# Three raw weight chunks in flight in a fused attention and two-layer-MLP kernel, with its conversion buffers placed elsewhere

## The chip, the cores and the metric

The kernel runs on one core of one Trainium2 chip. The metric is the device time of one execution in microseconds (us); before the change the median of three timed runs is 530.14 us.

## The reference

Attention with a tanh cap over 2 x 12 heads, 448 tokens, head size 64; then a layer of 1024 columns with a softmax gate and a layer norm; then a gated layer of 1536 columns. The weights arrive as 64-bit floats.

```python
scores = cap * np.tanh(scale * np.matmul(q, kT) / cap)
attn = np.exp(scores - max); attn = attn / (sum + 1e-09)
x = np.matmul(attn, v)                      # -> [896, 768]
h = x @ w_in                                # 768 -> 1024
solu = h * softmax(h)
x = (layernorm(solu) * g_ln) @ w_out        # 1024 -> 768
gate = sigmoid(x @ w_gate); val = x @ w_val # 768 -> 1536 each
out = gate * val @ w_out2                   # 1536 -> 768
```

## The kernel before

Four stages follow one another on TensorE (PE): attention with the start of the first layer beside it, the rest of the first layer, the second layer, the gated layer with the output product. Matmuls of the layers are done three times each, on a high and a low part of both operands (`hi`, `lo`).

**Attention.** The heads go in 12 pairs, each pair in two halves, so there are 24 *slots* (the loop over `s`, L533). In a slot ScalarE (ACT) takes the tanh of two tiles (L197), then their exp (L219); below, tanh 0 to tanh 23 number the slots by their tanh. PE does the scores of a half (`s_mm`, L191, 8 matmuls with both chunks), the product with v (`s_pv`, L237) and the sums of the exponentials (L245; for the pairs of `ADD_PAIRS`, 9 and 10, VectorE (DVE) first adds two tiles, L231, and PE sums half as often, L243). After a pair `s_out` copies the sums (DVE, L252) and the output (ACT, L253, tile `to`, 2 buffers), sends the sums through DMAs (L258); `n_recip` inverts them and spreads them over the partitions by two more DMAs (L266, L268); `n_mult` (GpSimd, POOL, L272) multiplies `to` by them two pairs later and so frees its buffer.

**Weights.** A chunk is 128 x 768 words of 64 bits (768 KB). `chunk_load` (L307) has the SP queue load it into `wraw` (2 buffers). Five word steps (L332 or, on ACT, L330; then on DVE L335, L336, L337, L338) make a 32-bit float out of it; L338 is the last reader of the raw chunk. The 8 chunks of `w_in` go through `cvt` and are split by L352 (ACT) and L355 (DVE); the 8 chunks of `w_mid` are made in place in tiles of the pool `w2a`. `chunk_stream` lays the steps of neighbouring chunks over each other:

```python
            steps[n - 1 - delay] = lambda f=f, c=c: (f(), load(c + AHEAD))
            order += [(n // 2 * c + k + (k >= n - delay), c, step) for k, step in enumerate(steps)]
```

For `w_mid` (five steps, delay 0) this puts step 5 of chunk c (L338) and the load of chunk c + AHEAD at the place of step 1 (L330) of chunk c + 2. `fill` hands the steps out evenly over the slots: `w_in` over slots 0 to S_WI, `w_mid` from S_WI to S_W2.

**Order.** PE, ACT, DVE and POOL run in the order in which the program names their instructions (`manual_schedule`, L459) up to L678; SP's order and everything behind L678 is the scheduler's. An engine works strictly in order.

**First layer.** Seven tiles of 128 tokens. Two run inside the attention, in thirds of 12 matmuls (L405): tile 0 in slots 17 to 19, tile 1 in slots 20 to 22. PSUM has three `big` buffers; scores take two in each slot, an accumulating tile takes one, and its buffer comes free only when DVE has done L423 (L415 max, L420 exp on ACT, L423 product). After the attention, tiles 2 to 6 go one by one.

**Gated layer.** `load_slabs` (L680) loads and converts two chunks (a *slab* each) for each of 12 steps, two steps ahead (`w4p`, 6 buffers; `w3p` for the first two), through `cvt` again; a step is 72 matmuls (L635). The output product has 6 steps of the same kind.

Of the kernel before, what the change touches and what calls it, by code (L numbers as in the profile page):

```python
# [20 lines left out]
P = 128  # L21
# [21 lines left out]
N_RAW = 3  # L43
AHEAD = 2

W2_EARLY = 4

ADD_PAIRS = range(9, 11)

# [3 lines left out]

S_WI = 14
S_W2 = 22
# [24 lines left out]
def fused_kernel(ctx: ExitStack, tc: tile.TileContext, qk, v, cap, w_in, w_mid, g_ln, w_gv, w_fin, outT):  # L80
# [4 lines left out]
    sh.pso = ctx.enter_context(tc.tile_pool(name="pso", bufs=2, space=PSUM))  # L85
    sh.wraw = ctx.enter_context(tc.tile_pool(name="wraw", bufs=2, side="right"))
    sh.cvt = ctx.enter_context(tc.tile_pool(name="cvt", bufs=2, side="right"))
    sh.dram = ctx.enter_context(tc.tile_pool(name="dram", bufs=2, space=DRAM))
# [52 lines left out]
def network(ctx: ExitStack, tc: tile.TileContext, sh, general, w_in, w_mid, w_gv, w_fin, outT):  # L141
    nc = tc.nc
    wide = w_in.dtype != F32
    wraw, cvt, ps, pso, ident = sh.wraw, sh.cvt, sh.ps, sh.pso, sh.ident
    sfx = "_g" if general else ""
# [11 lines left out]

    lin2 = lns.enter_context(tc.tile_pool(name="lin2" + sfx, bufs=2, side="right"))
    wi, x0 = ExitStack(), ExitStack()
    wip = wi.enter_context(tc.tile_pool(name="wi" + sfx, bufs=1, side="left"))  # L160
    x1p = wi.enter_context(tc.tile_pool(name="x1" + sfx, bufs=1, side="left"))
    x0p = x0.enter_context(tc.tile_pool(name="x0" + sfx, bufs=1, side="left"))
    wi_hi = wip.tile([P, 2, K1, 512], F32R, name="wi_hi")
# [57 lines left out]
    def s_pv(i, u):  # L221

        if u == 0:
            outs[i] = pso.tile([P, 512], F32, tag="o", name="o"), pso.tile([P, 512], F32, tag="o", name="sums")
        o, sums = outs[i]
        e = [es.pop((2 * i + j, u)) for j in range(2)]
        add = i in ADD_PAIRS and not general
        if add:
            for j in range(2):
                t = a3.tile([KC, S], F32, tag="es", name="es", bufs=4)  # L230
                nc.vector.tensor_tensor(t, e[j][:, 0], e[j][:, 1], ALU.add)  # L231
                es_sums.append(t)
        for c in range(2):
            kc = 2 * u + c
            for j in range(2):
                d = slice(j * D, j * D + D)
                nc.tensor.matmul(o[d, :S], vs[i][:, kc, d], e[j][:, c], start=(kc == 0), stop=(kc == 3))  # L237
        if add and u == 0:
            return
        for k in range(4):  # L240
            d = slice(k * 32, (k + 1) * 32)
            if add:
                nc.tensor.matmul(sums[d, :S], sh.ones, es_sums[k // 2 + k % 2 * 2], start=True, stop=True)  # L243
            else:
                nc.tensor.matmul(sums[d, :S], sh.ones, e[k // 2][:, k % 2], start=(u == 0), stop=(u == 1))  # L245
        es_sums.clear()

    def s_out(i):
        o, sums = outs.pop(i)
        t = a2.tile([P, S], F32, tag="to", name="to")  # L250
        st = a2.tile([P, S], F32, tag="ts", name="ts", bufs=1)
        (nc.vector.tensor_copy if i < NPAIR - 1 else nc.scalar.copy)(st, sums[:, :S])  # L252
        nc.scalar.copy(t, o[:, :S])  # L253
        tos[i] = t, st
        if i < NPAIR - 1:
            rs[i] = a2.tile([2 * RP, 2, RN], F32, tag="r", name="r")
            for c in range(2):
                nc.sync.dma_start(out=rs[i][:, c], in_=st[32 * c::D].rearrange("j (p n) -> j p n", n=RN))  # L258
# [14 lines left out]

    last, es_sums = {}, []

# [64 lines left out]

    def chunk_steps(get, dst, act=False):

        st = {}

        def place():
            st["w"] = cvt.tile([P, CH], U32, tag="cvt", name="cvt")
            return st["w"]
# [126 lines left out]
    wi_srcs = [w_in[:, c * CH:(c + 1) * CH] for c in range(K1 * F1 // CH)]  # L474
    chunk_stream(wi_srcs, lambda c, get: chunk_steps(get, wi_dst(c)), 1)

# [56 lines left out]
    for s in range(-1, NS):  # L533
# [25 lines left out]
        for first, end in ((0, S_WI), (S_WI, S_W2)):  # L559
            if first <= s < end:  # L560
                fill(-(-len(todo) // (end - s)))
        if u and i >= 2:
            n_mult(i - 2)
        if u and s > 0 and i < NPAIR - 1:
# [5 lines left out]
        if u == 0:  # L570
            v_load(i + 1)
        else:
            if i >= 1:
                n_recip(i - 1)
        if s < NS - 1:
            phase(s, 2)
            phase(s, 3)
# [102 lines left out]
    def load_slabs(src, pool):  # L680
# [3 lines left out]
        for c in range(src.shape[1] * P // CH):  # L684
            hl = pool.tile([P, 2, CH // P, P], F32R, tag="w", name="w_hl")
            parts = hl[:, 0].rearrange("p a b -> p (a b)"), hl[:, 1].rearrange("p a b -> p (a b)")
            r = chunk_load(flat[:, c * CH:(c + 1) * CH])
            for step in chunk_steps(lambda: r, lambda: parts, act=True):
                step()
            out.append(hl)  # L690
# [5 lines left out]


    w3p = ctx.enter_context(tc.tile_pool(name="w3p" + sfx, bufs=2, side="left", reuse_waits="tile"))
    w3 = [load_slabs(w_gv[0], w3p)]
    lns.close()  # L700
    w4p = ctx.enter_context(tc.tile_pool(name="w4p" + sfx, bufs=6, side="right", reuse_waits="tile"))
    w3 += [load_slabs(w_gv[1], w4p)]
# [73 lines left out]
```

## Time and profile before

| | us |
|---|---|
| median of three timed runs | 530.14 |
| lowest and highest of them | 528.61 and 530.21 |
| profiled execution: its time | 528.39 |
| profiled execution: its span | 526.5 |
| PE busy in the span | 499.9 (95%) |
| DVE busy | 312.0 (59%) |
| ACT busy | 234.6 (45%) |
| POOL busy | 55.8 (11%) |

All times of instructions are counted from the span's start; the execution's own time is 1.9 us longer than its span. Shares of the whole span say little here, since the four stages have different limits; they are read stage by stage.

### The profile page before, as it was taken

The numbers are of one execution on the slowest core, as the hardware profiler recorded it, in microseconds if no ns is written. First come the engines' busy times: TensorE is split into PE (matmuls) and PEld (weight loads), VectorE is DVE, ScalarE is ACT, GpSimd is POOL, SyncE is SP. The second block draws the span as 40 slices with busy tenths as digits, with TensorE's granted clock in tenths as the row PEclk, the third lists the DMA queues.
The fourth block names the chain that finished last, engine by engine and source line by source line (L and its number), as shares of the span: only waits on it lengthen the run. The fifth ranks groups of instructions, "written<-read, shape, count | busy, mean of one in ns | idle before, by whom it ended". The sixth has DMA issues, their size and how long they took to land.

```text
span 526.5 us, 6251 instructions
## 1 busy us (share of the span) xinstructions
PE 499.9 (95%) x2480; PEld 386.6 (73%) x2480; DVE 312.0 (59%) x424; ACT 234.6 (45%) x288; POOL 55.8 (11%) x41
## 2 busy tenths in 40 slices
PE   8998998879789889999999999999999999999996
PEld 4332232435366668988899999999999999999995
DVE  0776556659967779321189988776667675551000
ACT  5998996667524545120154433333333333332000
POOL 0011100002221110000001111111101111000000
PEclk9999998998999999999999999999999999999999
DMA  7567645442620000300033453333332234400001
GB/s 268 171 186 219 216 142 187 150 140 78 194 82 1 0 2 0 121 0 1 0 117 124 132 168 121 119 121 120 121 115 82 104 121 138 154 37 22 33 35 40
DMA packets 15313, 55.03 MB, mean 105 GB/s; under 512 B 2796, under 2 KB 5740, under 8 KB 15276
## 3 DMA queue, kind: packets, MB, share of 16 engines
q1 hardware_dynamic: 15276, 54.56, 32.3%
q8 instruction: 21, 0.34, 0.3%
q14 instruction: 16, 0.13, 0.1%
HBM read 51.68 MB, written 2.79 MB: 103 GB/s over the span
## 4 chain that ended last, share of the span: by engine, by line
PE 67%; DVE 12%; ACT 11%; DMA 6%; issue 2%; POOL 1%; SPq 0%; ACTq 0%; POOLq 0%; DVEq 0%
PE big L635 36%; PE l4o L635 16%; PE l2o L635 8%; DMA w_raw<-in_w_mid 4%; ACT e L197 4%; ACT e L219 3%; PE o L237 2%; DVE e L423 1%; PE big L191 1%; PE big L405 1%; DVE st L415 1%; DVE w_lo L527 1%; ACT e L441 1%; ACT e L420 1%; DVE lnlo L456 1%
## 5 line engine op out<-in xcount | busy, mean ns | idle before, releaser
L635 PE MATMUL big<-y_hi,w_hl 128*128 128x448 f32 x576 | 162.2, 362 | 0.0
L635 PEld LDWEIGHTS big<-y_hi,w_hl 128*128 128x128 f32 x576 | 108.0, 187 | 7.0
L635 PE MATMUL big<-y_lo,w_hl 128*128 128x448 f32 x288 | 104.5, 363 | 0.0
L635 PE MATMUL l4o<-p_hi,w_hl 128*128 128x448 f32 x288 | 80.7, 362 | 0.0
L635 PEld LDWEIGHTS big<-y_lo,w_hl 128*128 128x128 f32 x288 | 54.1, 188 | 4.5
L635 PEld LDWEIGHTS l4o<-p_hi,w_hl 128*128 128x128 f32 x288 | 54.0, 187 | 3.3
L355 DVE TENSOR_TENSOR w_hl<-cvt,w_hl 128x768 fp32r<-128x768 f32 x36 | 35.6, 993 | 32.0 <-ACT w_hl L352 31.8
L635 PE MATMUL l4o<-p_lo,w_hl 128*128 128x448 f32 x144 | 52.0, 362 | 0.0
L335 DVE TENSOR_SCALAR cvt<-cvt 128x768 f32<-128x768 f32 x44 | 36.4, 829 | 23.7 <-ACT cvt L330 23.2
L352 ACT CAST w_hl<-cvt 128x768 fp32r<-128x768 f32 x36 | 29.7, 831 | 45.6 <-PE big L635 30.3
L197 ACT ACTIVATE e<-big,cap_inv 112x896 f32<-112x896 f32 x48 | 46.0, 1018 | 6.0 <-PE big L191 5.9
L237 PE MATMUL o<-e,v 112*64 112x448 f32 x192 | 44.7, 556 | 3.7 <-ACT to L253 3.5
L219 ACT ACTIVATE e<-e,cap_abs 112x896 f32<-112x896 f32 x48 | 47.6, 1054 | 0.0
L725 POOL TENSOR_TENSOR p_lo<-sg,p_hi 128x896 fp32r<-128x896 f32 x12 | 25.8, 2153 | 203.3 <-ACT p_hi L724 203.3
L191 PE MATMUL big<-qk_raw 64*112 64x448 f32 x192 | 45.8, 578 | 1.0 <-DVE st L429 0.7
L330 ACT ACTIVATE cvt<-w_raw 128x768 f32<-128x768 f32 x36 | 32.2, 900 | 31.3 <-DVE w_hl L355 15.6
L337 DVE SCALAR_TENSOR_TENSOR cvt<-w_raw,cvt 128x768 uint32<-128x768 uint32 x44 | 43.0, 979 | 1.0
L338 DVE SCALAR_TENSOR_TENSOR cvt<-w_raw,cvt 128x768 uint32<-128x768 uint32 x44 | 42.9, 978 | 1.0
L191 PEld LDWEIGHTS big<-qk_raw 64*112 64x112 f32 x192 | 17.0, 179 | 28.3 <-issue 20.9
L405 PE MATMUL big<-wi_hi,xl 128*128 128x512 f32 x84 | 33.8, 402 | 4.1 <-POOL xl L393 3.3
L237 PEld LDWEIGHTS o<-e,v 112*64 112x64 f32 x192 | 13.6, 136 | 31.5 <-ACT e L219 13.3
L405 PE MATMUL big<-wi_hi,xh 128*128 128x512 f32 x84 | 34.7, 413 | 1.7 <-ACT xh L392 1.7
(98 smaller groups left out, 607.5 us busy)
## 6 DMA issues: line engine op xcount, KB each, us to landing
w_raw<-in_w_gv SPq DMA_DIRECT2D x24, 768.0 KB, 4.7
w_raw<-in_w_fin SPq DMA_DIRECT2D x12, 768.0 KB, 4.3
w_raw<-in_w_in SPq DMA_DIRECT2D x8, 768.0 KB, 5.9
w_raw<-in_w_mid SPq DMA_DIRECT2D x8, 768.0 KB, 4.6
qk_raw<-in_qk SPq DMA_DIRECT2D x12, 448.0 KB, 5.5
v<-in_v SPq DMA_DIRECT2D x12, 224.0 KB, 2.6
out_t<-ob SPq DMA_DIRECT2D x12, 224.0 KB, 2.3
qk_raw<-rd SPq DMA_DIRECT2D x22, 112.0 KB, 3.2
```

The source lines that it names most:

```text
L191: nc.tensor.matmul(sc[j][:KC, c, :S], r[d, 1, kc * KC:(kc + 1) * KC], r[d, 0], start=True, stop=True)
L197: nc.scalar.activation(e, es[n, u][:KC, :, :S], AF.Tanh, scale=sh.cap_inv[:KC])
L219: nc.scalar.activation(es[n, u], es[n, u], AF.Exp, scale=sh.cap_abs[:KC])
L237: nc.tensor.matmul(o[d, :S], vs[i][:, kc, d], e[j][:, c], start=(kc == 0), stop=(kc == 3))
L330: first = lambda t, lo, hi: nc.scalar.activation(f32(t), f32(hi), AF.Abs)
L335: word(lambda t, lo, hi: v.tensor_scalar(f32(t), f32(t), as_f32(W_MOST), as_f32(W_LEAST), ALU.min, ALU.max)),
L337: word(lambda t, lo, hi: v.scalar_tensor_tensor(t, hi, TOP, t, ALU.bitwise_and, ALU.bitwise_or)),
L338: word(lambda t, lo, hi: v.scalar_tensor_tensor(t, lo, 29, t, ALU.logical_shift_right, ALU.bitwise_or)),
L352: nc.scalar.copy(st["hi"], st["w"])
L355: nc.vector.tensor_tensor(st["lo"], st["w"], f32(st["hi"]), ALU.subtract)
L405: nc.tensor.matmul(hts[t][:, half], l[:, kk], r[:, half, kk], start=(kk == 0 and m == 0), stop=(kk == K1 - 1 and m == 2))
L635: nc.tensor.matmul(out, l, r, start=(first and m == 0), stop=(last and m == 2))
```

## The change

- `wraw` gets 3 buffers in place of 2, and `AHEAD` is 3 in place of 2, so that three raw chunks can be loaded or waiting.
- `cvt` is no longer one pool for the whole kernel. The `w_in` chunks are converted in tiles of `w2a`, which the `w_mid` chunks use later. The gated layer has a `cvt` of its own, which lies where the first layer's weights lay and so can be written only after the last matmul that reads those.
- `lin2` (tiles of the first layer) moves to the left side of SBUF and is freed with the first layer's weights; `w4p` has 5 buffers in place of 6.
- `ADD_PAIRS` goes: all pairs sum their exponentials on PE.
- `to` has 3 buffers in place of 2, and `n_mult` is named after `n_recip` in its slot.
- `S_WI` is 13 in place of 14: `w_in` is done, and `w_mid` begun, a slot earlier.

```diff
--- before.py
+++ after.py
@@ -41,17 +41,15 @@
 
 N_E = 5
 N_RAW = 3
-AHEAD = 2
+AHEAD = 3
 
 W2_EARLY = 4
-
-ADD_PAIRS = range(9, 11)
 
 L1_BESIDE = 2
 S_L1 = 16
 L1_SLOTS = 3
 
-S_WI = 14
+S_WI = 13
 S_W2 = 22
 WARM = 20
 ORDERED = {mybir.EngineType.PE, mybir.EngineType.Activation, mybir.EngineType.DVE, mybir.EngineType.Pool}
@@ -83,8 +81,7 @@
     const = ctx.enter_context(tc.tile_pool(name="const", bufs=1))
     sh.ps = ctx.enter_context(tc.tile_pool(name="ps", bufs=3, space=PSUM))
     sh.pso = ctx.enter_context(tc.tile_pool(name="pso", bufs=2, space=PSUM))
-    sh.wraw = ctx.enter_context(tc.tile_pool(name="wraw", bufs=2, side="right"))
-    sh.cvt = ctx.enter_context(tc.tile_pool(name="cvt", bufs=2, side="right"))
+    sh.wraw = ctx.enter_context(tc.tile_pool(name="wraw", bufs=3, side="right"))
     sh.dram = ctx.enter_context(tc.tile_pool(name="dram", bufs=2, space=DRAM))
 
 
@@ -141,7 +138,7 @@
 def network(ctx: ExitStack, tc: tile.TileContext, sh, general, w_in, w_mid, w_gv, w_fin, outT):
     nc = tc.nc
     wide = w_in.dtype != F32
-    wraw, cvt, ps, pso, ident = sh.wraw, sh.cvt, sh.ps, sh.pso, sh.ident
+    wraw, ps, pso, ident = sh.wraw, sh.ps, sh.pso, sh.ident
     sfx = "_g" if general else ""
 
     def big():
@@ -155,10 +152,10 @@
     ln_hi[0] = lnt1.tile([P, K2, G1], F32R, name="lnhi0")
     ln_lo[0] = lnt1.tile([P, K2, G1], F32R, name="lnlo0")
 
-    lin2 = lns.enter_context(tc.tile_pool(name="lin2" + sfx, bufs=2, side="right"))
     wi, x0 = ExitStack(), ExitStack()
     wip = wi.enter_context(tc.tile_pool(name="wi" + sfx, bufs=1, side="left"))
     x1p = wi.enter_context(tc.tile_pool(name="x1" + sfx, bufs=1, side="left"))
+    lin2 = wi.enter_context(tc.tile_pool(name="lin2" + sfx, bufs=2, side="left"))
     x0p = x0.enter_context(tc.tile_pool(name="x0" + sfx, bufs=1, side="left"))
     wi_hi = wip.tile([P, 2, K1, 512], F32R, name="wi_hi")
     wi_lo = wip.tile([P, 2, K1, 512], F32R, name="wi_lo")
@@ -224,30 +221,18 @@
             outs[i] = pso.tile([P, 512], F32, tag="o", name="o"), pso.tile([P, 512], F32, tag="o", name="sums")
         o, sums = outs[i]
         e = [es.pop((2 * i + j, u)) for j in range(2)]
-        add = i in ADD_PAIRS and not general
-        if add:
-            for j in range(2):
-                t = a3.tile([KC, S], F32, tag="es", name="es", bufs=4)
-                nc.vector.tensor_tensor(t, e[j][:, 0], e[j][:, 1], ALU.add)
-                es_sums.append(t)
         for c in range(2):
             kc = 2 * u + c
             for j in range(2):
                 d = slice(j * D, j * D + D)
                 nc.tensor.matmul(o[d, :S], vs[i][:, kc, d], e[j][:, c], start=(kc == 0), stop=(kc == 3))
-        if add and u == 0:
-            return
         for k in range(4):
             d = slice(k * 32, (k + 1) * 32)
-            if add:
-                nc.tensor.matmul(sums[d, :S], sh.ones, es_sums[k // 2 + k % 2 * 2], start=True, stop=True)
-            else:
-                nc.tensor.matmul(sums[d, :S], sh.ones, e[k // 2][:, k % 2], start=(u == 0), stop=(u == 1))
-        es_sums.clear()
+            nc.tensor.matmul(sums[d, :S], sh.ones, e[k // 2][:, k % 2], start=(u == 0), stop=(u == 1))
 
     def s_out(i):
         o, sums = outs.pop(i)
-        t = a2.tile([P, S], F32, tag="to", name="to")
+        t = a2.tile([P, S], F32, tag="to", name="to", bufs=3)
         st = a2.tile([P, S], F32, tag="ts", name="ts", bufs=1)
         (nc.vector.tensor_copy if i < NPAIR - 1 else nc.scalar.copy)(st, sums[:, :S])
         nc.scalar.copy(t, o[:, :S])
@@ -271,7 +256,7 @@
         b, hp = divmod(i, NP)
         nc.gpsimd.tensor_tensor(x_sb[b][:, hp], tos.pop(i)[0], sh.first[i % 2][:, 0], ALU.mult)
 
-    last, es_sums = {}, []
+    last = {}
 
     def n_by_pe(i, step):
 
@@ -338,12 +323,12 @@
             word(lambda t, lo, hi: v.scalar_tensor_tensor(t, lo, 29, t, ALU.logical_shift_right, ALU.bitwise_or)),
         ]
 
-    def chunk_steps(get, dst, act=False):
+    def chunk_steps(get, dst, pool, act=False):
 
         st = {}
 
         def place():
-            st["w"] = cvt.tile([P, CH], U32, tag="cvt", name="cvt")
+            st["w"] = pool.tile([P, CH], U32, tag="w", name="w_32")
             return st["w"]
 
         def upper():
@@ -472,7 +457,7 @@
         raws[i] = sh.first[i]
         load_qk(i + 2)
     wi_srcs = [w_in[:, c * CH:(c + 1) * CH] for c in range(K1 * F1 // CH)]
-    chunk_stream(wi_srcs, lambda c, get: chunk_steps(get, wi_dst(c)), 1)
+    chunk_stream(wi_srcs, lambda c, get: chunk_steps(get, wi_dst(c), w2a), 1)
 
 
     beside = {}
@@ -559,8 +544,6 @@
         for first, end in ((0, S_WI), (S_WI, S_W2)):
             if first <= s < end:
                 fill(-(-len(todo) // (end - s)))
-        if u and i >= 2:
-            n_mult(i - 2)
         if u and s > 0 and i < NPAIR - 1:
             s_out(i)
         if m % 2 and m < NS:
@@ -572,6 +555,8 @@
         else:
             if i >= 1:
                 n_recip(i - 1)
+            if i >= 2:
+                n_mult(i - 2)
         if s < NS - 1:
             phase(s, 2)
             phase(s, 3)
@@ -685,7 +670,7 @@
             hl = pool.tile([P, 2, CH // P, P], F32R, tag="w", name="w_hl")
             parts = hl[:, 0].rearrange("p a b -> p (a b)"), hl[:, 1].rearrange("p a b -> p (a b)")
             r = chunk_load(flat[:, c * CH:(c + 1) * CH])
-            for step in chunk_steps(lambda: r, lambda: parts, act=True):
+            for step in chunk_steps(lambda: r, lambda: parts, cvt, act=True):
                 step()
             out.append(hl)
         return out
@@ -695,10 +680,11 @@
         return [w[k // n][:, z, k % n] for z in range(2)]
 
 
+    cvt = ctx.enter_context(tc.tile_pool(name="cvt" + sfx, bufs=2, side="left", reuse_waits="tile"))
     w3p = ctx.enter_context(tc.tile_pool(name="w3p" + sfx, bufs=2, side="left", reuse_waits="tile"))
     w3 = [load_slabs(w_gv[0], w3p)]
     lns.close()
-    w4p = ctx.enter_context(tc.tile_pool(name="w4p" + sfx, bufs=6, side="right", reuse_waits="tile"))
+    w4p = ctx.enter_context(tc.tile_pool(name="w4p" + sfx, bufs=5, side="right", reuse_waits="tile"))
     w3 += [load_slabs(w_gv[1], w4p)]
     ptp = ctx.enter_context(tc.tile_pool(name="ptp" + sfx, bufs=1, side="left", reuse_waits="tile"))
     p_hi = ptp.tile([P, K4, NT], F32R, name="p_hi")
```

**The order of instructions.** The line numbers of the changed kernel are 3 to 15 lower (L197 is L194 there, L253 is L238, L310 is L295, L330 is L315, L335 is L320, L338 is L323, L423 is L408); names are the same.

SP's queue around the last `w_mid` loads. Before, from the sixth load (two loads in the first row) to the next sums behind the first gated loads:

```order
L310 DMA w_raw<-in_w_mid 128x1536 x2
L181 DMA v<-in_v 112x512
L258 DMA r<-ts 16x1x56 x2
L266 DMA rd<-r 16x56
L268 DMA qk_raw<-rd 64x448 x2
L310 DMA w_raw<-in_w_mid 128x1536
L310 DMA w_raw<-in_w_gv 128x1536 x2
L258 DMA r<-ts 16x1x56 x2
```

After, from the sixth load:

```order
L295 DMA w_raw<-in_w_mid 128x1536
L253 DMA qk_raw<-rd 64x448 x2
L95 DMA qk_raw<-in_qk 128x896
L295 DMA w_raw<-in_w_mid 128x1536
L178 DMA v<-in_v 112x512
L243 DMA r<-ts 16x1x56 x2
L251 DMA rd<-r 16x56
L253 DMA qk_raw<-rd 64x448 x2
L295 DMA w_raw<-in_w_mid 128x1536
L178 DMA v<-in_v 112x512
L295 DMA w_raw<-in_w_gv 128x1536
L243 DMA r<-ts 16x1x56 x2
```

The last load of `w_mid` moves from behind the last pair's v load and a pair's sums to ahead of that v load.

ACT around tanh 16, the slot in which the `w_mid` stream first needs ACT. Before, from tanh 14 to the start of tanh 17:

```order
L197 ACTIVATE e<-big,cap_inv 112x896 x2
L219 ACTIVATE e<-e,cap_abs 112x896 x2
L352 CAST wi_hi<-cvt 128x768
L253 COPY to<-o 128x448
L197 ACTIVATE e<-big,cap_inv 112x896 x2
L219 ACTIVATE e<-e,cap_abs 112x896 x2
L197 ACTIVATE e<-big,cap_inv 112x896 x2
L219 ACTIVATE e<-e,cap_abs 112x896 x2
L330 ACTIVATE w_w<-w_raw 128x768
L253 COPY to<-o 128x448
L197 ACTIVATE e<-big,cap_inv 112x896 x2
```

After, from the cast ahead of tanh 14 to the start of tanh 17:

```order
L337 CAST wi_hi<-w_568 128x768
L194 ACTIVATE e<-big,cap_inv 112x896 x2
L216 ACTIVATE e<-e,cap_abs 112x896 x2
L238 COPY to<-o 128x448
L194 ACTIVATE e<-big,cap_inv 112x896 x2
L216 ACTIVATE e<-e,cap_abs 112x896 x2
L315 ACTIVATE w_w<-w_raw 128x768
L194 ACTIVATE e<-big,cap_inv 112x896 x2
L216 ACTIVATE e<-e,cap_abs 112x896 x2
L315 ACTIVATE w_w<-w_raw 128x768
L238 COPY to<-o 128x448
L194 ACTIVATE e<-big,cap_inv 112x896 x2
```

The first absolute value (L330, chunk 2 of `w_mid`) moves from behind tanh 16 to ahead of it, the second (chunk 3) from behind tanh 17 to ahead of it; casts and copies no longer fall into the same slot.

DVE around the product of first-layer tile 0 (L423, in the changed kernel L408), with buffer numbers. Before (w2_w_939 is chunk 6):

```order
L393 TENSOR_TENSOR xl_957<-x0_161,xh_956 128x768
L415 TENSOR_REDUCE st_960<-big_839 128x1
L231 TENSOR_TENSOR es_976<-e_916 112x448
L231 TENSOR_TENSOR es_978<-e_918 112x448
L335 TENSOR_SCALAR w2_w_939<-w2_w_939 128x768
L338 SCALAR_TENSOR_TENSOR w2_w_891<-w_raw_888,w2_w_891 128x768
L336 TENSOR_SCALAR w2_w_939<-w2_w_939 128x768
L337 SCALAR_TENSOR_TENSOR w2_w_939<-w_raw_936,w2_w_939 128x768
L423 TENSOR_TENSOR e_972<-big_839,e_972 128x1024
```

After (w2_w_934 is chunk 6, w2_w_984 chunk 7):

```order
L378 TENSOR_TENSOR xl_954<-x0_158,xh_953 128x768
L400 TENSOR_REDUCE st_957<-big_845 128x1
L321 TENSOR_SCALAR w2_w_934<-w2_w_934 128x768
L322 SCALAR_TENSOR_TENSOR w2_w_934<-w_raw_826,w2_w_934 128x768
L320 TENSOR_SCALAR w2_w_984<-w2_w_984 128x768
L408 TENSOR_TENSOR e_969<-big_845,e_969 128x1024
```

The two adds are gone; the second word step of chunk 7 (L335, now L320), which needs that chunk's absolute value from ACT, now stands ahead of the product.

## Rows read from the trace of the kernel before

**Rows 1.** Windows: length; PE, PEld, DVE, ACT, POOL busy; TensorE clock; DMA share; GB/s.

```profile
0.00:79.80 79.80, 75.85 (x398) 27.14 (x400) 47.04 (x81) 69.29 (x82) 7.77 (x11) 1.00 0.64 200
79.80:148.90 69.10, 59.14 (x276) 27.87 (x276) 50.44 (x74) 44.32 (x54) 10.75 (x7) 0.95 0.47 153
117.70:122.00 4.30, 4.29 (x13) 2.31 (x14) 3.58 (x6) 3.95 (x6) 0.00 (x0) 0.64 0.14 53
148.90:201.50 52.60, 44.98 (x209) 34.91 (x208) 38.48 (x63) 22.74 (x30) 10.85 (x10) 1.00 0.02 5
201.50:262.60 61.10, 61.09 (x309) 54.75 (x310) 20.30 (x33) 13.80 (x21) 0.55 (x1) 1.00 0.07 26
262.60:526.50 263.90, 258.85 (x1292) 241.90 (x1291) 155.76 (x175) 84.47 (x104) 25.84 (x12) 1.00 0.32 101
```

**Rows 2.** Waits of ACT, 46 to 149 us: total us, times, longest.

```profile
ACT w_w L330 <- DMA w_raw<-in_w_mid: 16.6, 6, 3.7
ACT to L253 <- POOL x L272: 4.9, 2, 2.6
...
ACT cvt L330 <- DMA w_raw<-in_w_gv: 1.9, 2, 1.1
```

**Rows 3.** Timeline of ACT: start, length, what; in brackets the idle time before it.

```profile
33.58 1.96 ACT L197 ACTIVATE e<-big,cap_inv 112x896 f32<-112x896 f32 x2
35.37 2.03 ACT L219 ACTIVATE e<-e,cap_abs 112x896 f32<-112x896 f32 x2
37.23 0.88 ACT L352 CAST wi_hi<-cvt 128x768 fp32r<-128x768 f32 x1
37.97 0.57 ACT L253 COPY to<-o 128x448 f32<-128x448 f32 x1
38.40 1.95 ACT L197 ACTIVATE e<-big,cap_inv 112x896 f32<-112x896 f32 x2
...
49.18 0.53 ACT L253 COPY to<-o 128x448 f32<-128x448 f32 x1 [2.59 <-POOL x L272]
...
79.77 1.91 ACT L197 ACTIVATE e<-big,cap_inv 112x896 f32<-112x896 f32 x2 [0.72 <-PE big L191]
...
102.59 0.90 ACT L330 ACTIVATE w_w<-w_raw 128x768 f32<-128x768 f32 x1 [3.72 <-DMA w_raw<-in_w_mid]
```

**Rows 4.** Timeline of DVE, then of SP, around two raw loads.

```profile
97.15 0.94 DVE L338 SCALAR_TENSOR_TENSOR w_w<-w_raw,w_w 128x768 uint32<-128x768 uint32 x1
...
98.16 0.33 SPq L310 DMA_DIRECT2D w_raw<-in_w_mid  x1
...
122.98 0.35 SPq L310 DMA_DIRECT2D w_raw<-in_w_mid  x1
```

**Rows 5.** Timeline of PE: a slot with first-layer matmuls, and the end of the attention.

```profile
99.30 1.76 PE L191 MATMUL big<-qk_raw 64*112 64x448 f32 x8
101.00 0.50 PE L405 MATMUL big<-wi_hi,xh 128*128 128x512 f32 x1
...
103.94 1.72 PE L237 MATMUL o<-e,v 112*64 112x448 f32 x8
105.59 1.94 PE L191 MATMUL big<-qk_raw 64*112 64x448 f32 x8
...
112.07 0.96 PE L243 MATMUL sums<-es,ones 112*32 112x448 f32 x8
...
117.71 0.60 PE L237 MATMUL o<-e,v 112*64 112x448 f32 x2 [2.99 <-ACT to L253]
...
148.92 0.62 PE L283 MATMUL big<-ident,ts 128*112 128x128 f32 x4
```

**Rows 6.** Timeline of DVE: the product of first-layer tile 0.

```profile
124.31 1.22 DVE L423 TENSOR_TENSOR e<-big,e 128x1024 f32<-128x1024 f32 x1
```

**Rows 7.** Timeline of DVE, in the second layer.

```profile
226.43 1.08 DVE L645 TENSOR_TENSOR y_lo<-l2o,y_hi 128x384 fp32r<-128x384 f32 x2 [5.02 <-ACT y_hi L644]
```

**Rows 8.** Chain of waits, in order of time: start, length, what.

```profile
228.48 11.09 PE l2o L635 x48
```

## The prediction, made before the changed kernel was run

> **What bounds the kernel now.** I read four views in this order: the windows by stage, the waits of ACT, the timelines of ACT, DVE, SP and PE, and the order of instructions on each engine.
>
> The windows cut the span into stages [rows 1]. From 201.5 us on PE is busy 61.09 of 61.10 us and then 258.85 of 263.90, the last two stages have no gap worth taking. Between 148.9 and 201.5 us the DMA share is 0.02: first-layer tiles run one by one there, and nothing that the change does to loads can touch them. So all that can move lies ahead of 148.9 us, where two stretches differ. Up to 79.8 us ACT is busy 69.29 of 79.80. From 79.8 to 148.9 us no engine is full: PE 59.14, DVE 50.44 and ACT 44.32 of 69.10, with the granted clock at 0.95. A stretch in which nobody is full is one of waits.
>
> The waits of ACT name them [rows 2]: 16.6 us in six waits of L330 for a raw `w_mid` chunk, 4.9 us in two waits of the copy L253 for POOL's product, 1.9 us for chunks of the gated layer. ACT works in order, so behind each L330 that waits stand the next tanh and with it the scores and all of PE. The timelines show why the chunk is late. DVE starts L338, the last reader of a raw buffer, at 97.15; SP issues the next load into that buffer at 98.16 [rows 4]; ACT, which came to its L330 3.72 us earlier, starts it at 102.59 [rows 3]. With two buffers and AHEAD 2 a load is issued at the place in the order where its own first step stands, so its 4.4 us (98.16 to 102.59) are hidden only by what ACT has left to do.
>
> **The change, part by part.** Slots are named by their tanh.
>
> *Until tanh 16.* The first wait of L253 is the 2.59 us at 49.18 [rows 3]: POOL's product, two pairs back, had not freed `to`. A third `to` buffer asks for the product of a pair earlier, and that wait goes. A slot on ACT, read start to start between 33.58 and 38.40 [rows 3], is 1.79 (two tanh), 1.86 (two exp), 0.74 if a cast falls into it, 0.43 if a copy does. Without the wait tanh 9 starts near 46.6 + 0.43 = 47.0. Seven slots to tanh 16 with three casts, three copies and, new there, one absolute value (0.79) are 7 x 3.65 + 3 x 0.74 + 3 x 0.43 + 0.79 = 29.9, so tanh 16 starts near 76.9 in place of 79.77 [rows 3]. I take **-2.8 us**. PE's slot, 1.70 + 1.65 + 0.89 = 4.24 (below), stays just under ACT's 4.3.
>
> *From tanh 16 to the end of the attention* (L283, 148.92 [rows 5]; 69.15 us now). With AHEAD 3 the load of chunk c + 3 is issued after L338 of chunk c, and its L330 stands one slot later than now. A slot is at least 4.8 us there and a load takes 4.4, so the six waits go. Then PE sets the pace. Its pieces, start to start [rows 5]: scores 1.70 (99.30 to 101.00), 12 first-layer matmuls 2.94 (101.00 to 103.94), v product 1.65 (103.94 to 105.59), sums 0.89 to 0.96 (112.07). Slot by slot:
> - 16 to 17, on ACT: 1.79 + 1.86 + 0.79 + 0.43 = 4.9; 17 to 18, with a split of x in place of the copy: 5.2.
> - 18 to 19: 1.70 + 2.94 and about 1.1 in which the third matmul waits for the low half of the split: 5.8.
> - 19 to 20 and 20 to 21, full on PE: 1.70 + 1.65 + 0.89 + 2.94 = 7.2 each.
> - 21 to 22: 7.2 and a **new wait of 2.0**. The scores of slot 22 need the `big` buffer that L423 frees. L423 now stands behind the L335 of the last chunk, which needs that chunk's L330, which stands on ACT behind exp 21. From the start of tanh 21: 1.8 for tanh, 1.1 for L420 (an estimate from 0.90 for 768 columns [rows 3]), 1.9 for exp, 0.8 for L330, 0.5 for L335, 1.2 for L423 [rows 6]: 7.3. PE has 1.65 + 0.89 + 2.94 = 5.4 of work meanwhile.
> - 22 to 23: 7.2. From tanh 23 on: half of it 0.9, transposes 0.8, 2.94, twice 2.54, 2.94: 12.7.
>
> The sum is 59.4, against 69.15: **-9.8 us**. In it are the second wait of L253 (2.28, gone), the two gated conversions that leave ACT and DVE here (1.9 of waits, 3 us of work on DVE), and the price of dropping `ADD_PAIRS`: two more rounds of sums, 2 x 0.89 on PE in full slots, while the eight adds leave DVE. A bound from the other side: PE's 59.14 busy us [rows 1] hold some 3 us of half clock and gain 1.8, so the stretch cannot fall below about 58, a gain of 11.2.
>
> *The clock.* Between 117.7 and 122.0 us it was granted at 0.64, that is a mix of the 1.2 and the 2.4 GHz level, in a spell in which PE had stood idle 2.99 us up to 117.71, waiting for ACT [rows 5]; 4.3 us at 0.64 lose 1.5. The new wait of 2.0 us may bring one such spell; I count half, **+0.7**, ends 0 and 1.5 twice.
>
> *Handovers* between engines cost about 0.1 each and are left out of the slots: **+0.5**, ends 0 and 1.5.
>
> *Conversions of the gated layer.* They now begin after the last first-layer matmul, at the end of its stage (201.50 before [rows 1]). In the second layer DVE stood idle 5.02 us ahead of the first y_lo (226.43, half of 1.08), whose bank PE wants at 228.48 [rows 7, 8]: 5.0 + 1.5 to spare. The order puts two splits and six word steps ahead, 2 x 0.95 + 4 x 0.55 + 2 x 0.95 = 6.0. **0**, ends 0 and 1.
>
> *Five slab buffers.* A step of the gated layer is 72 matmuls of 258.85 / 1292 = 0.20 us, 14.4 us [rows 1]. The second slab of step n + 2 must now wait until the first of step n is read, in the middle of step n; it is wanted 28.8 us later. The cast that waits there stands on ACT ahead of a sigmoid that becomes ready at the same moment: 0.8 us late, with half a step, 7.2 us, of a free PSUM buffer before PE asks. **0**. If that cover went, each of 12 steps would lose 0.8.
>
> *Start.* Three `w_in` loads now stand ahead of the second v load. The first stretch moves 200 GB/s [rows 1], so 768 KB more is at most 3.9 us; that v chunk is the one of the third pair, ahead of whose product stand four slots of some 4.2. **0**, ends 0 and 1.
>
> Sum: -2.8 - 9.8 + 0.7 + 0.5 = -11.4, from 528.39 to 517.0. The profiled execution is the fastest of the four shown; the timed three lie 0.2 to 1.8 above it, so a median should come out about 1 higher: **518 us**.
>
> **The rivals.**
> 1. *The loads stay late.* SP is in order too, and loads stand behind copies that wait for DMAs (L268 behind L266). What speaks against this change is a rule of the Trainium skill, in "SBUF — State Buffer", section "Can I just issue two DMAs to hit both halves?": all of a kernel's DMAs land on the same 16 engines, and two at once serialize, so a third chunk in flight adds no rate. If the stream were short of rate, the 16.6 us would stay and only the two waits for POOL go: 528.4 - 2.8 - 2.3 = 523.3, with the 1 us for the median 524.3. By that rule the time would be this; the trace does not bear it out here, since the DMA share of the stretch is 0.47 [rows 1], and a stretch of 59 us would need 0.55. What is missing is an earlier start, not rate.
> 2. *The freed time is taken elsewhere* (half clock after more PE gaps, scores waiting for `big` buffers in several slots): no change, 529 to 531. Against it: PE has 10 us free in the stretch [rows 1].
> 3. *Slower: the new wait decides.* L423 now needs the last chunk's L330. If that chunk's load were issued as late as now, at 122.98 [rows 4], it would land at 127.4, where the forecast has L330 at about 112.6; the difference goes one to one into the wait for the `big` buffer: 518 + 14.8, near 532. It turns the sign once the chunk lands later than about 124. For it: the load stands behind L268 in SP's queue. Against it: it needs only L338 of the fifth chunk, by the slots above two slots ahead of its own L330, some 14 us earlier, against 4.4 for the load.
>
> **How the numbers follow.** Forecast (514 to 521.5: below, 11.2 in place of 9.8 and some 2.6 less still if neither clock nor handovers cost anything and slots of the first stretch come out 0.2 shorter, 7 x 0.2; above, the ends of clock, handovers, y_lo and start) 0.62; loads stay late, wholly or in part (521.5 to 525) 0.23; no gain 0.09; slower 0.06. A measurement of this kernel can tell about 0.3%, 1.6 us, from no change, so the first two cases are faster: 0.85, with 0.09 and 0.06 behind them. The range 514 to 524.5 holds the first and most of the second.
>
> **What would show it.** Waits of L330 for `in_w_mid` of nearly 0, none of L253 for POOL; tanh 16 near 77; slots 19 to 23 about 7 us apart with PE full; one PE wait of some 2 us that ends on L423 or the small statistics behind it, near 114; L283 near 137; the stages behind it as long as before. The forecast is wrong if L330 still waits for DMAs, if the clock share of the stretch falls, or if PE shows gaps behind 201.5 us less the gain.

## The result, and the profile after

The changed kernel took 516.86 us (median of 4 runs, 515.58 to 517.64) against 529.6 us before (now 4 runs): a ratio of 0.976, 95% interval 0.973 to 0.979. The profiled execution took 517.01 us with a span of 515.2, that is 11.3 us of span less.

The windows of the changed kernel, cut at tanh 16, at the end of the attention (now L268), at the first matmuls of the second layer and of the gated layer, with the columns of [rows 1]:

```profile
0.00:78.50 78.50, 74.87 (x398) 27.32 (x400) 52.72 (x86) 70.25 (x83) 10.65 (x11) 1.00 0.67 214
78.50:138.30 59.80, 57.36 (x292) 26.79 (x293) 35.25 (x53) 42.78 (x52) 9.23 (x7) 1.00 0.48 153
138.30:190.90 52.60, 44.99 (x210) 34.90 (x208) 38.49 (x63) 22.00 (x28) 10.83 (x10) 1.00 0.00 1
190.90:251.40 60.50, 60.50 (x309) 54.68 (x310) 25.61 (x41) 15.60 (x23) 0.55 (x1) 1.00 0.16 53
251.40:515.20 263.80, 258.59 (x1293) 241.94 (x1291) 155.74 (x175) 84.98 (x104) 25.69 (x12) 1.00 0.31 98
```

Against [rows 1] the stretch of the `w_mid` stream fell from 69.10 to 59.80 us, and PE, busy 59.14 of the 69.10, is now busy 57.36 of the 59.80. The first stretch lost 1.3 us, the stages behind 138.3 us together 0.7. The waits of ACT from 46 to 140 us, as in [rows 2]:

```profile
ACT e L194 <- PE big L188: 10.8, 6, 3.4
ACT e L405 <- DVE st L400: 2.2, 1, 2.2
ACT to L238 <- PE o L228: 1.6, 1, 1.6
...
```

No wait for `w_raw` is left, none of the copy (L238) for POOL. ACT now waits for scores, that is for PE. The new wait that the prediction put near 114 us is there. DVE, PE and then DVE again, from the timelines of the changed kernel:

```profile
114.74 0.56 DVE L320 TENSOR_SCALAR w_w<-w_w 128x768 f32<-128x768 f32 x1 [2.45 <-ACT w_w L315]
115.21 1.22 DVE L408 TENSOR_TENSOR e<-big,e 128x1024 f32<-128x1024 f32 x1
116.35 0.14 DVE L414 TENSOR_SCALAR st<-st 128x1 f32<-128x1 f32 x1
...
116.48 1.75 PE L188 MATMUL big<-qk_raw 64*112 64x448 f32 x6 [1.26 <-DVE st L414]
```

DVE stands at the second step of the last chunk (L320) until ACT has made its absolute value; L408 is behind it, and the scores of slot 22 behind L408. Slots 19 to 22, from the starts of tanh 19 to 23 (94.44, 101.62, 108.84, 117.54, 125.45), are 7.18, 7.22, 8.70 and 7.91 us long: the two long ones are the slot with this wait and the one behind it.

### The profile page after: what moved, and what is told of

Read it like the earlier page. It is cut to its first block, busy times and chain, and to the rows that moved or that the text cites. A ratio compares the mean times of both kernels' runs of the same rounds, so it can differ in the third digit from the quotient of the medians.

```text
span 515.2 us, 6254 instructions
## 1 busy us (share of the span) xinstructions
PE 496.3 (96%) x2496; PEld 385.6 (75%) x2496; DVE 307.8 (60%) x416; ACT 235.6 (46%) x288; POOL 57.0 (11%) x41
## 4 chain that ended last, share of the span: by engine, by line
PE 82%; ACT 8%; DVE 7%; issue 1%; POOL 1%; DMA 0%; ACTq 0%; POOLq 0%
PE big L620 37%; PE l4o L620 17%; PE l2o L620 8%; PE o L228 7%; PE big L188 6%; PE big L390 3%; PE sums L231 3%; ACT e L194 2%; ACT e L216 2%; DVE e L408 1%; DVE st L400 1%; DVE w_lo L512 1%; ACT e L405 1%; ACT e L426 1%; DVE lnlo L441 1%
## 5 line engine op out<-in xcount | busy, mean ns | idle before, releaser
L337 ACT CAST w_hl<-w 128x768 fp32r<-128x768 f32 x36 | 29.8, 834 | 91.0 <-PE big L620 77.0
L340 DVE TENSOR_TENSOR w_hl<-w,w_hl 128x768 fp32r<-128x768 f32 x36 | 34.2, 954 | 32.9 <-ACT w_hl L337 32.9
L194 ACT ACTIVATE e<-big,cap_inv 112x896 f32<-112x896 f32 x48 | 46.1, 1021 | 16.1 <-PE big L188 16.1
L320 DVE TENSOR_SCALAR w<-w 128x768 f32<-128x768 f32 x44 | 37.8, 860 | 24.9 <-ACT w L315 24.3
L188 PE MATMUL big<-qk_raw 64*112 64x448 f32 x192 | 44.4, 563 | 1.6 <-DVE st L414 1.3
L323 DVE SCALAR_TENSOR_TENSOR w<-w_raw,w 128x768 uint32<-128x768 uint32 x44 | 43.9, 998 | 1.0
L322 DVE SCALAR_TENSOR_TENSOR w<-w_raw,w 128x768 uint32<-128x768 uint32 x44 | 43.7, 996 | 1.0
L315 ACT ACTIVATE w<-w_raw 128x768 f32<-128x768 f32 x36 | 32.3, 903 | 15.3 <-DVE w_hl L340 14.8
L188 PEld LDWEIGHTS big<-qk_raw 64*112 64x112 f32 x192 | 16.0, 174 | 28.7 <-issue 21.8
```

The costliest lines, as they stand in the source:

```text
L188: nc.tensor.matmul(sc[j][:KC, c, :S], r[d, 1, kc * KC:(kc + 1) * KC], r[d, 0], start=True, stop=True)
L194: nc.scalar.activation(e, es[n, u][:KC, :, :S], AF.Tanh, scale=sh.cap_inv[:KC])
L315: first = lambda t, lo, hi: nc.scalar.activation(f32(t), f32(hi), AF.Abs)
L320: word(lambda t, lo, hi: v.tensor_scalar(f32(t), f32(t), as_f32(W_MOST), as_f32(W_LEAST), ALU.min, ALU.max)),
L322: word(lambda t, lo, hi: v.scalar_tensor_tensor(t, hi, TOP, t, ALU.bitwise_and, ALU.bitwise_or)),
L323: word(lambda t, lo, hi: v.scalar_tensor_tensor(t, lo, 29, t, ALU.logical_shift_right, ALU.bitwise_or)),
```

## Experiments

Before took 528.04 us beside the first two groups of runs and 527.75 beside the last. "Stretches" are those of each profile from tanh 0 to tanh 16 and from there to the end of the attention; counted so, the start, which moves by up to 1.6 us from run to run, stays out. Before has 71.96 and 69.15, the changed kernel 70.52 and 59.86.

| run | us | ratio to before, 95% | stretches |
|---|---|---|---|
| changed kernel again | 517.32 | 0.980 (0.978 to 0.983) | 71.26, 61.50 |
| two_raw | 528.78 | 1.002 (1.000 to 1.003) | 73.96, 64.09 |
| ahead2 | 516.50 | 0.980 (0.976 to 0.984) | 71.27, 59.87 |
| to2 | 519.51 | 0.985 (0.982 to 0.988) | 71.34, 61.05 |
| only_three | 516.01 | 0.978 (0.975 to 0.980) | 71.10, 58.01 |
| swi14 | 513.93 | 0.974 (0.972 to 0.976) | 70.18, 57.87 |
| add_pairs | 516.33 | 0.978 (0.976 to 0.981) | 69.74, 59.86 |
| he_early | 513.57 | 0.973 (0.972 to 0.975) | 70.50, 57.60 |
| he_s14 | 512.25 | 0.970 (0.967 to 0.972) | 69.53, 57.61 |
| he_s14_to2 | 515.26 | 0.975 (0.972 to 0.978) | 71.96, 57.99 |
| he_s14_to2_add2 | 517.78 | 0.980 (0.978 to 0.983) | 72.62, 59.26 |
| he_s14_to2_add4 | 522.84 | 0.989 (0.986 to 0.992) | 73.00, 64.96 |

### The third raw buffer, and the place of the load

The first puts both numbers back:

```diff
-AHEAD = 3
+AHEAD = 2
-name="wraw", bufs=3
+name="wraw", bufs=2
```

> The changed kernel with two raw buffers and AHEAD 2 again, all else kept. Theory A (the gain is that each w_mid load is issued a slot earlier in the order): the six waits of ACT for w_raw come back, 12 to 17 us in all, the attention's end moves from 138.3 to about 146, the time is 522 to 526 us. Theory B (the gain comes from the other parts: the third output buffer, the sums, the moved conversions): within 1 us of 517 us, no such waits. Theory C (rate of the DMA engines was short, a third chunk adds none): also within 1 us of 517.

The second only the one:

```diff
-AHEAD = 3
+AHEAD = 2
```

> Three raw buffers but AHEAD 2: a load has a free buffer earlier, but its place in the order is that of two in flight. Theory A (place of the issue decides, SP has nothing else to wait for): the same as with two raw buffers, within 1.5 us of it, since a load still stands behind L338 two chunks before its own. Rival A2 (the buffer is what made the load wait: with a third buffer free, SP can issue without waiting for L338): close to the changed kernel, 517 to 519 us, waits of ACT for w_raw under 4 us in all.

With two buffers the whole gain is gone, more than expected: 528.78 us. Its profiled execution, 524.09, was the fastest of the ten, so its rows show the kind of wait, not its full size. Waits of ACT from 20 to 150 us with two buffers:

```profile
ACT w_w L315 <- DMA w_raw<-in_w_mid: 11.8, 4, 4.1
```

With three buffers and AHEAD 2 nothing is lost. My reason, a load that stands a slot earlier in the order, fell; rival A2 holds: SP, whose order is the scheduler's, does not wait for the place at which a load is named, only for the buffer. Apart from one load at the start, SP's queue in the attention is the same with either value. The fourth to sixth of the eight `w_mid` loads on SP's timeline with two buffers:

```profile
83.06 0.33 SPq L295 DMA_DIRECT2D w_raw<-in_w_mid  x1
90.27 0.35 SPq L295 DMA_DIRECT2D w_raw<-in_w_mid  x1
98.73 0.33 SPq L295 DMA_DIRECT2D w_raw<-in_w_mid  x1
```

The same three with three buffers and AHEAD 2:

```profile
75.83 0.35 SPq L295 DMA_DIRECT2D w_raw<-in_w_mid  x1
78.63 0.33 SPq L295 DMA_DIRECT2D w_raw<-in_w_mid  x1
84.47 0.35 SPq L295 DMA_DIRECT2D w_raw<-in_w_mid  x1
```

And in the changed kernel:

```profile
76.43 0.35 SPq L295 DMA_DIRECT2D w_raw<-in_w_mid  x1
79.55 0.33 SPq L295 DMA_DIRECT2D w_raw<-in_w_mid  x1
85.21 0.35 SPq L295 DMA_DIRECT2D w_raw<-in_w_mid  x1
```

The sixth load is issued at 84.47 and 85.21 us with three buffers, whatever AHEAD is, and at 98.73 with two.

### The output buffers, and the rest of the change

In to2 the third output buffer goes, and the product stands ahead of the copies again:

```diff
-        t = a2.tile([P, S], F32, tag="to", name="to", bufs=3)
+        t = a2.tile([P, S], F32, tag="to", name="to")
+        if u and i >= 2:
+            n_mult(i - 2)
         if u and s > 0 and i < NPAIR - 1:
             s_out(i)
...
-            if i >= 2:
-                n_mult(i - 2)
```

> Two output buffers to again, with the product of two pairs back named ahead of the copies as before; all else kept. Theory A: ACT's copy waits for POOL's product twice again, near 48 us and in the second half, 2.2 to 2.6 us each; the first costs 1.8 us of the end of the attention, the second is partly covered by PE's work, so 518.5 to 521 us. Rival (the third buffer buys nothing, the wait only stands elsewhere): within 1 us of 517.

only_three has this edit too, and beside it the ADD_PAIRS and S_WI 14 of before:

```diff
-S_WI = 13
+S_WI = 14
+ADD_PAIRS = range(9, 11)
...
+        add = i in ADD_PAIRS and not general
+        if add:
+            for j in range(2):
+                t = a3.tile([KC, S], F32, tag="es", name="es", bufs=4)
...
```

> Of the change only three raw chunks in flight and the conversion buffers' new places (with five slab buffers): two output buffers, ADD_PAIRS on pairs 9 and 10 and S_WI 14 as before the change. Theory A: nearly the whole gain of the stretch with w_mid remains, 519 to 522 us, no waits of ACT for w_raw. Theory B (the other parts carry the gain): 525 us or more.

Two output buffers cost 2.2 us against the changed kernel on the same chip (517.32 to 519.51), as the theory had it, though the intervals of the two ratios just touch; ACT's copy waits for POOL four times in this profile, not twice, 0.5 to 2.1 us each (4.4 in all). Yet only_three, which has two as well, is faster by 1.3 us than the whole change, and by 3 or more than was expected of it. So some part of the rest costs time. The next runs look for it, swi14 and he_early by one line each:

```diff
-S_WI = 13
+S_WI = 14
```

```diff
-        at(s1 + 1, 2, ln_he, t)
+        at(s1 + 1, 1, ln_he, t)
```

> The changed kernel once more, on the chip on which its variants run: a ratio of 0.976 to before, within 0.003. It is what the other three are compared with.

> The changed kernel with S_WI 14 again. Theory: S_WI decides little; the 0.5 us that a cast of w_in waits for DVE near 38 us goes, and w_mid's steps still find their chunks loaded, since the third buffer and not the place of the steps hides the load: within 1 us of the changed kernel, waits of ACT for w_raw under 1.5 us. Rival (w_mid's earlier start is what removed the waits): 2 us or more slower, with waits for w_raw back.

> The changed kernel with the product of first-layer tiles 0 and 1 (L408) named right behind its exponential, ahead of the slot's word steps, so that it no longer stands behind the last chunk's second step. Theory: PE's wait of 1.26 us for the big buffer near 116 us goes and the time falls by 1.3, to about 515.5. Rival (the exponential itself comes too late, or the transposes behind wait longer instead): within 0.5 us of the changed kernel.

The changed kernel came out at a ratio of 0.980 this time, a little outside what was expected. Of the other three, add_pairs is taken up under "The sums".

swi14 and he_early took away the same thing and gave 3.4 and 3.8 us. With S_WI 14 the last chunk's second step moves behind L408, with he_early L408 moves ahead of it; in either profile PE has no wait behind L414, tanh 21 to tanh 22 takes 7.17 us in place of 8.70, and the second stretch is 2.0 and 2.3 us shorter. For S_WI I had expected nothing: I had not seen that it is S_WI that puts that step there; from he_early I had expected 1.3. S_WI 14 alone does not rule the wait out: in only_three DVE's adds stand ahead of the product, and PE waits 1.22 us there too.

The medians differ by more than the stretches, and the clock bears on the rest. The five executions of the changed kernel on this chip took 516.30 and 516.47 us at a granted clock of 1.00, 517.32 at 0.997, 519.17 and 519.28 at 0.994. The profiled one is that of 519.17. PE's wait in it, and the window behind, with the columns of [rows 1]:

```profile
117.12 1.75 PE L188 MATMUL big<-qk_raw 64*112 64x448 f32 x6 [1.26 <-DVE st L414]
...
118.00:123.40 5.40, 5.40 (x18) 3.51 (x17) 4.59 (x8) 3.76 (x4) 4.02 (x3) 0.68 0.31 76
```

The wait is as long as in the first profile, but here the clock fell behind it, to 0.68, a mix of the 1.2 and the 2.4 GHz level; slot 22 took 9.50 us where it had taken 7.91, and the stretch 61.50. The ten executions of swi14 and he_early, without the wait, all have 0.997 or more. So part of their gain is likely this spell, which followed the wait in one profile and not in the other; what decides it no run shows. DVE's timeline with he_early, the product at once behind ACT's exponential:

```profile
111.20 1.23 DVE L408 TENSOR_TENSOR e<-big,e 128x1024 f32<-128x1024 f32 x1 [1.27 <-ACT e L405]
112.34 0.55 DVE L321 TENSOR_SCALAR w_w<-w_w 128x768 uint32<-128x768 uint32 x1
```

The last group begins with he_s14, which has the edits of swi14 and he_early together. he_s14_to2 adds the edit of to2, he_s14_to2_add2 also the ADD_PAIRS of only_three (pairs 9 and 10), and he_s14_to2_add4 has

```diff
-ADD_PAIRS = range(9, 11)
+ADD_PAIRS = range(8, 12)
```

> The changed kernel with both: the product L408 named early and S_WI 14. Theory: both took away one and the same wait (L408 behind the last chunk's second step), so together they give no more than one alone: within 1 us of 513.6, a ratio of 0.973 to before. Rival (two independent gains of 3.4 and 3.7 us): 510 to 511 us, a ratio under 0.968.

> The same with two output buffers to. Theory: the two waits of ACT's copy for POOL's product come back, 1.5 to 3 us slower than with three buffers. Rival (where PE sets the pace the copy's wait is covered, and in the first stretch PE catches up): within 0.7 us of the kernel with three.

512.25 us, a ratio of 0.970 to before, is the fastest of all. Against he_early it is faster by some 2 us (ratios 0.970 and 0.973, on two chips), between the two expectations: the second stretch does not change (57.60 and 57.61), so there it was one wait, as the theory said, but the first is 1.0 us shorter. Of this, 0.8 us lie from tanh 6 to tanh 8, where a cast of he_early waits 0.5 us for DVE (8.46 and 9.28 us). That wait does not hang on S_WI: the profiles of two_raw, to2 and add_pairs, with S_WI 13, do not have it, and those of swi14 and he_s14_to2, with 14, do. What brings it is shown in the last section. So the rows show no gain of both edits over one, and where the 2 us between the medians come from is open.

Two output buffers cost 3.0 us here. In the first stretch, 2.4 us longer, 0.8 are that cast's wait, which he_s14 does not have, and 1.7 the copy's (tanh 8 to 9: 6.52 and 4.79). ACT's timeline in he_s14_to2, the two copies that wait:

```profile
49.10 0.53 ACT L238 COPY to<-o 128x448 f32<-128x448 f32 x1 [1.61 <-POOL x L257]
...
124.59 0.53 ACT L238 COPY to<-o 128x448 f32<-128x448 f32 x1 [3.36 <-POOL x L257]
```

And POOL's, ahead of the second:

```profile
120.14 2.62 POOL L428 TENSOR_SCALAR e<-e,st 128x1024 f32<-128x1024 f32 x1 [0.35 <-DVE st L424]
122.73 1.83 POOL L257 TENSOR_TENSOR x<-to,qk_raw 128x448 f32<-128x448 f32 x1
```

The second wait isn't one for the sums' way through DMAs: POOL's product stands behind the layer norm of tile 0 (L428), which ends late.

### The sums

> The same with two output buffers and ADD_PAIRS as before the change, all four sums of a pair made at once. Theory: pairs 9 and 10 stand where PE is full, so 2 x 0.89 = 1.8 us faster than without. Rival (other waits take the time): within 0.7 us.

> The same with ADD_PAIRS on pairs 8 to 11. Theory: 0.89 us for each pair whose sums PE makes where it is full; pair 8 falls half into a slot that ACT sets, pair 11 into the end, so 2.5 to 3.6 us faster than without ADD_PAIRS. Rival (DVE's adds, in order with the word steps and the layer norm, come too late): no faster than with two pairs.

Both theories failed, in sign; the rival of the second held. The price itself is right: tanh 19 to 20 and 21 to 22 take 6.29 us with two pairs added, 7.18 without. But slot 22 to 23 grows from 7.56 to 10.65. ACT's timeline there, in he_s14_to2_add2:

```profile
126.94 0.53 ACT L252 COPY to<-o 128x448 f32<-128x448 f32 x1 [6.45 <-POOL x L271]
```

And POOL's:

```profile
121.37 3.75 POOL L442 TENSOR_SCALAR e<-e,st 128x1024 f32<-128x1024 f32 x1 [0.35 <-DVE st L438]
125.09 1.82 POOL L271 TENSOR_TENSOR x<-to,qk_raw 128x448 f32<-128x448 f32 x1
```

The copy comes earlier, the product later, and with two output buffers the copy holds up tanh 23; the 1.8 us go and 3.1 are paid. That is 1.3 of the 2.5 us between the medians; 0.7 more lie in the first stretch, ahead of the two pairs. With pairs 8 to 11 added, the same wait stands, and two waits of PE for DVE's adds are new (2.2 us in all); the slots that hold them are 2.9 and 2.8 us longer, and the stretch was granted a clock of 0.97. ADD_PAIRS as before beside three output buffers was not run; in its place, add_pairs has a form in `s_pv` that needs three buffers for the added tiles:

```diff
+        add = i in ADD_PAIRS and not general
+        if add:
+            ts = [a3.tile([KC, S], F32, tag="es", name="es", bufs=3) for j in range(2)]
+            for j in range(2):
+                nc.vector.tensor_tensor(ts[j], e[j][:, 0], e[j][:, 1], ALU.add)
...
+        if add:
+            for j in range(2):
+                d = slice(64 * j + 32 * u, 64 * j + 32 * u + 32)
+                nc.tensor.matmul(sums[d, :S], sh.ones, ts[j], start=True, stop=True)
+            return
```

> The changed kernel with the sums of pairs 9 and 10 added by DVE first again (three buffers for the added tiles instead of four, each half summed in its own slot, so that they fit beside the third output buffer). Theory: PE sets the pace of the second stretch, so two rounds of sums less on PE, 2 x 0.89 us, come off the time: 1.8 us faster than the changed kernel, 514.5 to 515.5 where that has 516.8. Rival (DVE's four adds per pair come late for PE, or the 2 us wait for the big buffer takes the time back): within 0.7 us of the changed kernel.

It came out near the rival, 1.0 us under the changed kernel with a second stretch of 59.86 as there (its first stretch is 0.8 shorter, without the cast's wait). PE did wait once for DVE's adds, 1.05 us, as the rival had it, but the chief reason neither had named: slots 19 and 20 take 7.17 and 7.21 us, as before this edit. PE's timeline in add_pairs:

```profile
98.42 0.95 PE L239 MATMUL sums<-es,ones 112*32 112x448 f32 x4
```

And in only_three, where all four sums are made at once:

```profile
104.80 0.96 PE L242 MATMUL sums<-es,ones 112*32 112x448 f32 x8
```

Four matmuls into two quarters of the columns take as long as eight into all four (the trace counts two for each of the program). Half the matmuls in each of two halves saves nothing; all four sums at once in one half, as before the change, saves a round of 0.89 us.

## Why the prediction was right, and where it was not

The forecast was 518 us, 517.0 for the profiled execution; it took 517.01 and the median is 516.86. Term by term, that is partly luck: the first stretch fell 1.5 us short, and 0.7 in the second and 0.7 behind it, neither forecast, made up for it.

- **Until tanh 16: -2.8 forecast, -1.3 found** (79.77 to 78.48). The wait of L253 went as said: tanh 8 to 9 takes 4.81 us where it took 7.55. The step that failed is the one behind it, tanh 9 "near 46.6 + 0.43 = 47.0" and then seven slots of ACT's own work, with no wait for DVE. Tanh 9 starts at 47.82, since a cast waits 0.5 us for a word step on DVE near 38 us that takes 1.91 us in place of 0.95; at 47.53 a step is late in the same way and the next cast 0.3 us behind it. Both steps run beside POOL's product (rows in the last section). At tanh 16 ACT waits 0.4 for scores. The seven slots were 30.7 us, not 29.9.
- **Tanh 16 to the end of the attention: -9.8 with +0.7 and +0.5, so -8.6 forecast, -9.3 found** (69.15 to 59.86). The slots came out as reckoned: PE's 7.2 us were 7.18 and 7.22. The clock term, half a spell, is nothing in this profile, where the stretch was granted 1.00, and a whole spell in the second, 1.6 us in a stretch granted 0.97, with PE's wait at 1.26 us in both. So the forecast of "may bring" was right, and which of the two came was luck.
- **The new wait: 2.0 forecast.** It shows as 1.26 us of PE and two slots that are 1.5 and 0.7 too long against the 7.2 reckoned; taking it away shortens the stretch by 2.0 to 2.3. The mechanism was right to the instruction; that S_WI 13 puts the step there, and could be dropped, was not said. The prediction gave S_WI no price.
- **AHEAD.** "With AHEAD 3 the load of chunk c + 3 is issued after L338 of chunk c" describes what the buffer allows. ahead2 shows that the number itself does nothing here.
- **ADD_PAIRS: 1.8 us for two pairs on PE** is what the slots show. As a price of the change it is not one: with the third output buffer that came in its place the kernel is faster, 513.93 (swi14) against 516.01 (only_three), with intervals that just touch.
- **Rival 1, no rate for a third chunk.** Ahead of it stood a rule of the Trainium skill ("SBUF — State Buffer", "Can I just issue two DMAs to hit both halves?"): two DMAs at once, measured there on tiles at partitions 0 and 64, serialize. The rows agree as far as the single load goes: the median `w_mid` load took 4.6 us before and 5.5 with three in flight. But the stretch used 0.48 of the DMA engines, and an earlier start hid the longer load; two_raw shows that it was the start that was missing.
- **Rival 3** had the wait in it that came, but not the late load: the last chunk was asked for at 98.14 us, where 122.98 was feared.
- **Nothing behind 148.9 us: forecast 0, found -0.7.** First-layer tiles and the gated layer with five slab buffers are as before (52.60 and 263.80 against 52.60 and 263.90). The second layer is 0.6 us shorter: the chain of waits has three groups of 48 matmuls at 10.92 or 10.93 us, where they took 11.09 or 11.10 [rows 8]. No run was made on the cause.

So, on the chip of the first two groups: the third raw buffer, with the conversions moved to make room for it, is worth 12.0 us (528.04 to 516.01), trading ADD_PAIRS for an output buffer 2.1 (to 513.93), and S_WI 13 gives 3.4 back (to 517.32). Of these three parts only the last cost time. The moved conversions and the five slab buffers were not run by themselves; two_raw, which has both, is no faster than before.

## What to carry to other kernels

When an engine that works in order waits for a load, look at what frees the buffer, not at where the load is named: if its queue is ordered by a scheduler, a third buffer alone moves the load. When steps are handed out evenly over slots, shifting the window by one slot moves every step; list what each step then stands ahead of on its engine, since one step that waits for another engine, ahead of a product that frees a PSUM buffer, cost 2.0 to 2.3 us of the stretch here, and in one of two profiles a spell of lower clock stood behind it. And price work taken off the bounding engine together with the next wait in its path: 1.8 us off PE turned into 3.1 us for a copy behind POOL.

## What was not expected of the hardware

Sums into two of the four 32-column quarters took 0.95 us, into all four 0.96 (the rows above): matmuls on different quarters run side by side, so leaving half of them out saves nothing. The Trainium skill has the first half of this ("TensorE: Matmul & The Clock Gate", "Part 3: Packing small matmuls — row/col tiling": small matmuls at different tile positions run at the same time in one array); the rows agree, and I had not thought of it when I wrote add_pairs.

DVE and POOL slowed each other. DVE's timeline in the changed kernel, the same step at two times and a step with one input between:

```profile
111.33 0.96 DVE L322 SCALAR_TENSOR_TENSOR w_w<-w_raw,w_w 128x768 uint32<-128x768 uint32 x1
...
119.98 0.55 DVE L321 TENSOR_SCALAR w_w<-w_w 128x768 uint32<-128x768 uint32 x1
120.57 1.76 DVE L322 SCALAR_TENSOR_TENSOR w_w<-w_raw,w_w 128x768 uint32<-128x768 uint32 x1
122.36 1.78 DVE L323 SCALAR_TENSOR_TENSOR w_w<-w_raw,w_w 128x768 uint32<-128x768 uint32 x1
```

And POOL's at the same time:

```profile
119.30 2.22 POOL L428 TENSOR_SCALAR e<-e,st 128x1024 f32<-128x1024 f32 x1 [0.35 <-DVE st L424]
121.49 1.84 POOL L257 TENSOR_TENSOR x<-to,qk_raw 128x448 f32<-128x448 f32 x1
```

The two steps that read two tensors of SBUF end about 0.8 us after POOL's two operations (122.33 and 124.14, against 121.52 and 123.33), that is almost a whole step after each. POOL's product takes 1.84 us here and 1.15 elsewhere (103.26 in he_s14_to2), its L428 2.22 here, 3.75 in he_s14_to2_add2 (L442 there) and 1.20 later in this kernel (144.19). A rule of the Trainium skill ("SBUF — State Buffer", "Who interferes with whom": a DVE instruction with two SBUF inputs and a POOL instruction that reads SBUF exclude each other, and the later waits for the whole of the other) fits these rows. The step with one input keeps its 0.55 here, but not always: L321 at 58.32 takes 1.40 beside POOL's product.

The same step and the same product at another place, first in the changed kernel, where POOL starts first:

```profile
35.84 1.39 POOL L257 TENSOR_TENSOR x<-to,qk_raw 128x448 f32<-128x448 f32 x1 [34.54 <-DVE w L322]
...
36.13 1.91 DVE L323 SCALAR_TENSOR_TENSOR w<-w_raw,w 128x768 uint32<-128x768 uint32 x1
```

Then in add_pairs, where DVE does:

```profile
36.38 0.95 DVE L335 SCALAR_TENSOR_TENSOR w<-w_raw,w 128x768 uint32<-128x768 uint32 x1
...
36.85 1.50 POOL L269 TENSOR_TENSOR x<-to,qk_raw 128x448 f32<-128x448 f32 x1 [35.55 <-DMA qk_raw<-rd]
```

With 1.91 us the cast behind it on ACT waits, with 0.95 it does not. Counted from tanh 0, DVE comes to this step at 28.2 us in each of the thirteen profiles of the changed kernel and its variants. POOL's first product starts at 27.7 to 28.1 in the eight that have the long step, four with S_WI 13 and four with 14, and at 28.3 to 28.7 in the five that do not. So it is this overlap that decides, and not S_WI. At 47.53 in the changed kernel the split L340 takes 1.90 us beside the next product (47.45). No run was made to take the overlap away.
